# Two heads' shared query tile weighed by the whole TensorE array, each head in a PSUM slot of its own

## The chip, the cores and the metric

The kernel runs on one core of a Trainium2 chip. The metric is the device time of one execution in microseconds (us). Before the change the median of three runs is 1435.6 us (1434.48 to 1436.16).

## What is computed

Three layers stand one behind the other. The first is attention over 4 batches and 8 heads with 1152 keys of 64 numbers, where neighbouring pairs of queries are averaged, so that 576 queries per head are left. Its output, 2304 rows of 512, goes through two feed-forward layers (512 to 2048 to 512), one with `h * cos(h)`, one with `h * sigmoid(h)`.

```python
q_pool = q.reshape(B, H, S // 2, 2, D).mean(axis=3)
scores = scale * np.matmul(q_pool, k.transpose(0, 1, 3, 2))
scores = scores - np.max(scores, axis=-1, keepdims=True)
attn = np.exp(scores)
attn = attn / (np.sum(attn, axis=-1, keepdims=True) + 1e-09)
x = np.matmul(attn, v)            # 576 queries x 64 for each of 32 heads
h = x_rows @ w_in;  g = h * np.cos(h);  y = g @ w_out          # layer 1
h = y @ w_in2;      g = h / (1 + np.exp(-h));  out = g @ w_out2 # layer 2
```

## The kernel before, in words

**Pairs and tiles.** The 32 heads are worked in 16 pairs. A head has 576 = 4 x 128 + 64 queries: four whole tiles of 128 queries, and half a tile. The two halves of a pair share one tile, so that a pair has nine tiles: eight of one head each and one, number 8 (`2 * NT`), whose rows 0 to 63 are queries of the first head and rows 64 to 127 queries of the second. There are 144 tiles in all.

**The way of a tile.** `tile_scores` multiplies the queries with the keys on TensorE (PE) into PSUM (`sp`; lines 390, and 398 for the shared tile). `tile_exp` moves the scores out on VectorE (DVE, line 409) and takes the exponential on ScalarE (ACT, line 417). `tile_hi` and `tile_lo` split the result into two float16 parts (`hl`; ACT line 423, GpSimd (POOL) line 428), and a DMA issued by SyncE (SP, line 430) transposes them into `hlT`. Four tiles later `tile_pv` (line 434) weighs the values: 9 chunks of 128 keys times three products of high and low parts, 27 matmuls of 64 or 65 columns into `pv` (line 442). Column 65 of `vt` is ones, so that the sum of the weights comes out beside the weighted values.

**The shared tile in `tile_pv`.** Its 128 columns of weights are cut into two halves. The loop of line 439 first runs all 27 matmuls with columns 0 to 63 of `hlT` as stationary operand and the first head's values, into partitions 0 to 63 of its slot, and then 27 with columns 64 to 127 and the second head's values, into partitions 64 to 127. That is 54 matmuls on half the array's columns. The score products of the shared tile (line 398) are cut in the same way, with the two heads taking turns.

**Groups.** Five tiles (`GT`) share one PSUM tile `pv`, one slot of 65 numbers each; a pair has a group of five, whose last is the shared tile, and a group of four. `group_end` (line 448) divides by the sums: two small DVE instructions make the reciprocals (lines 451, 455), and line 461 multiplies each destination: `x` for whole tiles, `xrem` for the shared one. There is one `pv` buffer, so the next group's first product waits for the last of these.

**The order.** The program is written tile by tile. Between tiles a generator puts in units of layer 1 (`g1_unit` line 518, `g2_unit1` line 578, 12 matmuls of 256 columns each) at a fixed rate once the first block of attention is done. The framework then orders each engine's instructions by priority and by simulated times; `tile_pv` has a lower urgency (`P_PV = -100`), so that its matmuls are mixed with those of layer 1 on PE. Each engine then works its list strictly in order. After the last tile come the rest of layer 1, with the second layer's weights being decoded, and layer 2 (lines 518 and 599).

Of the kernel before, what the change touches and what calls it, by code (L numbers as in the profile page):

```python
# [11 lines left out]
F32 = mybir.dt.float32  # L12
# [28 lines left out]
GT = 5  # L41
# [3 lines left out]
def attention_moe_moe_kernel(ctx, tc, q, k, v, w_in1, w_out1, w_in2, w_out2, out):  # L45
# [4 lines left out]
    B, H, S, D = q.shape  # L50
# [6 lines left out]
    NT = SQ // 128  # L57
# [5 lines left out]
    small = ctx.enter_context(tc.tile_pool(name="small", bufs=2))  # L63
# [49 lines left out]
    @contextmanager  # L113
    def ahead(n):

        at_ = tc.cur_priority
        tc.cur_priority = at_ - n
        yield
        tc.cur_priority = at_ + (tc.cur_priority - (at_ - n))
# [147 lines left out]
    def att_pools(stack):  # L267
        at = Weights()
        at.p = stack.enter_context(tc.tile_pool(name="att", bufs=2, side="right", reuse_waits="tile"))
        at.src_stack = ExitStack()  # L270
        at.src = at.src_stack.enter_context(tc.tile_pool(name="src", bufs=2, side="right", reuse_waits="tile"))
        at.ps_s = stack.enter_context(tc.tile_pool(name="ps_s", bufs=1, space=PSUM, side="right"))
        at.ps_v = stack.enter_context(tc.tile_pool(name="ps_v", bufs=1, space=PSUM, side="right"))
        return at
# [102 lines left out]
    def tile_scores(at, P, t):  # L377


        T = Pair()  # L380
        T.P, T.t = P, t

        parts = [(0, 512), (512, S)]
        T.sp = [(a, z, at.ps_s.tile([128, z - a], F32, tag="sp%d" % a, name="sp")) for a, z in parts]
        if t < 2 * NT:
            kT = P.kT[t // NT]
            for a, z, sp in T.sp:
                for o, n in segs:
                    for e in range(2 if a <= o < z else 0):
                        nc.tensor.matmul(  # L390
                            sp[:, o - a:o - a + n], P.qT[e][:, t, :], kT[:, o:o + n], start=(e == 0), stop=(e == 1)
                        )
        else:
            for a, z, sp in T.sp:
                for o, n in segs:
                    for e in range(2 if a <= o < z else 0):
                        for i in range(2):
                            nc.tensor.matmul(
                                sp[i * 64:(i + 1) * 64, o - a:o - a + n], P.qT[e][:, t, i * 64:(i + 1) * 64],
                                P.kT[i][:, o:o + n], start=(e == 0), stop=(e == 1),  # L400
                            )
        return T
# [31 lines left out]
    def tile_pv(at, T):  # L434
        P, t, G = T.P, T.t, T.G
        if T.gi == 0:
            G.pv = at.ps_v.tile([128, GT, D + 1], F32, tag="pv", name="pv")
        hs = [(slice(0, 128), t // NT)] if t < 2 * NT else [(slice(0, 64), 0), (slice(64, 128), 1)]
        for r, i in hs:
            for c in range(KC):  # L440
                for e, z, n in ((0, 0, D + 1), (0, 1, D), (1, 0, D + 1)):
                    nc.tensor.matmul(  # L442
                        G.pv[r, T.gi, 0:n], T.hlT[:, e, c, r], P.vt[i][:, c, z, 0:n],
                        start=(c == 0 and e == 0 and z == 0), stop=(c == KC - 1 and e == 1),
                        skip_group_check=True,
                    )

    def group_end(at, G, n, dsts):

        den = small.tile([128, GT, 1], F32, tag="den", name="den", bufs=2)  # L450
        nc.vector.tensor_scalar(
            out=den[:, 0:n], in0=G.pv[:, 0:n, D:D + 1], scalar1=1e-9 * 2.0**PSH, scalar2=G.P.s[:, 2:3],
            op0=ALU.add, op1=ALU.mult,
        )
        nc.vector.reciprocal(den[:, 0:n], den[:, 0:n])
        for o, shape, dst in dsts:
            k = math.prod(shape)
            src, d = G.pv[:, o:o + k, 0:D], den[:, o:o + k].to_broadcast([128, k, D])
            if len(shape) == 2:
                src, d = (x.rearrange("p (t a) d -> p t a d", a=shape[1]) for x in (src, d))  # L460
            nc.vector.tensor_tensor(out=dst, in0=src, in1=d, op=ALU.mult)
# [154 lines left out]
    if True:  # L616
# [3 lines left out]
        xrem = wpool.tile([128, B, NP * D], F32, name="xrem")  # L620

        att_stack = ExitStack()
        at = att_pools(att_stack)
# [19 lines left out]
        def finish(g):  # L643
            while g in bg:
                advance()
# [45 lines left out]
        P = {}  # L691
# [36 lines left out]
        def x_of(b, i):  # L728
            if (b, i) not in x32:
                if (b - 1, i) in xgens:  # L730
                    finish(xgens[b - 1, i])
                x32[b, i] = wpool.tile([128, 2, DM], F32, tag="x32_%d" % i, name="x32")
            return x32[b, i]

        def block_done(b, i):
            if state.mp is None:
                finish(wg)
                wst_stack.close()
                state.mp = moe_pools(moe_stack)
            xgens[b, i] = block_steps(b, i)  # L740
            bg.append(xgens[b, i])

        def drain_pv():
            T = inflight.pop(0)
            G = T.G
            with ahead(P_PV):
                tile_pv(at, T)
            if T.gi < len(G.tiles) - 1:
                return
            b, j = T.P.b, T.P.j  # L750
            dsts = []
            if j < NP - 1:
                h = j + (G.tiles[0] // NT) * NP
                for i in range(2):
                    dsts.append((2 * i, (2,), x_of(b, i)[:, :, h * D:(h + 1) * D]))
            else:
                x = x_of(b, G.tiles[0] % NT // 2).rearrange("p t (a h d) -> p t a h d", a=2, d=D)
                dsts.append((0, (2, 2), x[:, :, :, j, :]))
            if G.tiles[-1] == 2 * NT:
                dsts.append((len(G.tiles) - 1, (1,), xrem[:, b:b + 1, j * D:(j + 1) * D]))  # L760
            group_end(at, G, len(G.tiles), dsts)
            if j == NP - 1:
                left[b] = left.get(b, set(range(2 * NT))) - set(G.tiles)
                for i in range(2):
                    if (b, i) not in gone and all(t % NT // 2 != i for t in left[b]):
                        gone.add((b, i))
                        block_done(b, i)
# [3 lines left out]
        for n, (b, j) in enumerate(pairs):  # L771
# [7 lines left out]
            for o in range(0, len(seq), GT):  # L779
                G = Pair()  # L780
# [9 lines left out]
            for idx, (G, gi, t) in enumerate(order):  # L790
                with ahead(P_SC):
                    T = tile_scores(at, P[n], t)
                T.G, T.gi = G, gi
                inflight.append(T)
                with ahead(P_EX):
                    tile_exp(at, T)
                tile_hi(at, T, b == 0 or (idx % HI_N) < HI_A)
                tile_lo(at, T)
                advance()
                share(RATE[b] / 2)  # L800
                advance()
                if len(inflight) > LAG:
                    drain_pv()
                advance()
                share(RATE[b] / 2)
                advance()
        while inflight:
            drain_pv()
            share(1)
# [23 lines left out]
        for i in range(2):  # L833
            T = wpool.tile([128, B, 2, 128], F16, tag="x32_%d" % i, name="xrT")
# [124 lines left out]
```

## Time and profile before

| | us |
|---|---|
| median of 3 runs | 1435.6 |
| profiled execution, whole | 1439.78 |
| its span in the trace | 1438.0 |
| PE busy | 1189.1 (83%) |
| DVE busy | 992.8 (69%) |
| ACT busy | 736.7 (51%) |
| POOL busy | 561.3 (39%) |

The profiled execution took 1.8 us more than its span and 4.2 us more than the median of the runs. Attention goes from the start to about 885 us, with layer 1 beside it from about 280 us on; the rest of layer 1 lasts until about 1036 us, layer 2 until the end. "Granted clock" is the share of TensorE's full clock that the chip gave; it has two levels, 2.4 GHz (1.0) and 1.2 GHz (0.5). In the forms of PE's instructions, 128*128 and 128*64 are rows and columns of the array in use. A matmul's duration in the trace runs from its start to its modelled end through the pipeline, some 0.19 us even for a small one; how long it holds the engine is seen from the start of the next.

### The profile page before, as it was taken

Reading aid. Unit: us, or ns where it says so; the run is one execution under the profiler, and the core shown is the slowest. Engines: PE = TensorE matmul, PEld = TensorE weight load, DVE = VectorE, ACT = ScalarE, POOL = GpSimd, SP = SyncE. Lnnn points to the kernel's source line nnn. Section 1 sums busy time; section 2 is a strip of 40 time slices with the busy share of each in tenths; the row PEclk is TensorE's granted clock in tenths of the full one; section 3 lists DMA queues with packets and bytes.
Section 4 is the critical chain, followed back from the end, with each engine's and each line's share of the span. In section 5 each row is a group of like instructions: output and inputs, shape, how many; then the busy total and the mean of one; then the engine's idle time right before and its main releaser. Section 6 shows DMA issues by size and latency. Waiting matters only on the chain. (4 is left out here: it accounts for less than half of the span.)

```text
span 1438.0 us, 27552 instructions
## 1 busy us (share of the span) xinstructions
PE 1189.1 (83%) x11460; PEld 870.2 (61%) x11460; DVE 992.8 (69%) x1840; ACT 736.7 (51%) x763; POOL 561.3 (39%) x264
## 2 busy tenths in 40 slices
PE   1455365779988877998979989898899999999998
PEld 0233244566766655676656768777786666666665
DVE  7999987598787867987798895999833222323212
ACT  3676486477667667776667665546511111111110
POOL 1578375454556474656645552545410000000000
PEclk9986568798999998999999999989899999999999
DMA  7799889986799999997997965434210000000001
GB/s 230 191 232 199 206 161 187 207 159 111 153 210 164 198 204 185 202 162 161 182 188 144 222 102 107 123 113 132 74 60 30 15 16 30 30 30 15 16 1 30
DMA packets 493085, 186.34 MB, mean 130 GB/s; under 512 B 433056, under 2 KB 467872, under 8 KB 492960
## 3 DMA queue, kind: packets, MB, share of 16 engines
q1 hardware_dynamic: 492960, 184.59, 62.5%
q8 instruction: 89, 1.46, 0.4%
q14 instruction: 36, 0.29, 0.1%
HBM read 66.58 MB, written 9.44 MB: 53 GB/s over the span
## 5 line engine op out<-in xcount | busy, mean ns | idle before, releaser
L428 POOL TENSOR_TENSOR hl<-sc,hl 128x1152 f16<-128x1152 f32 x144 | 368.0, 2564 | 221.9 <-ACT hl L423 132.6
L442 PE MATMUL pv<-vt,hlT 128*128 128x65 f16 (+3 forms) x4320 | 253.5, 206 | 61.6 <-DMA hlT<-hl 45.2
L442 PEld LDWEIGHTS <-hlT 128*128 128x128 f16 (+1 forms) x4320 | 208.2, 108 | 119.0 <-DMA hlT<-hl 57.3
L518 PEld LDWEIGHTS <-ih 128*128 128x128 f16 x2304 | 226.4, 99 | 75.1 <-issue 14.9
L390 PE MATMUL sp<-kT,qT 128*128 128x512 f16 (+1 forms) x768 | 193.0, 366 | 95.1 <-DVE sc L409 77.7
L409 DVE TENSOR_SCALAR_CACHE_REDUCE sc<-sp,psu 128x512 f32<-128x512 f32 (+1 forms) x288 | 229.9, 808 | 52.1 <-PE sp L390 43.3
L531 ACT ACTIVATE hk<-h,ca 128x512 f32<-128x512 f32 x144 | 98.2, 683 | 326.8 <-PE h L518 326.8
L417 ACT ACTIVATE sc<-sc,nb 128x1152 f32<-128x1152 f32 x144 | 179.8, 1251 | 152.2 <-DVE nb L414 129.0
L518 PE MATMUL h<-ys,ih 128*128 128x256 f16 x1152 | 197.4, 274 | 2.9 <-ACT hk L531 2.9
L518 PE MATMUL h<-xT,ih 128*128 128x256 f16 x1024 | 190.6, 278 | 7.9 <-DVE pu__2739 L98 3.4
L423 ACT ACTIVATE hl<-sc 128x1152 f16<-128x1152 f32 x144 | 165.6, 1157 | 19.3 <-DMA hlT<-hl 11.7
L566 DVE TENSOR_SCALAR gh<-hk,ck 128x1024 f16<-128x1024 f32 x36 | 27.0, 751 | 206.9 <-PE o L599 194.2
L390 PEld LDWEIGHTS <-qT 128*128 128x128 f16 x768 | 76.3, 108 | 153.3 <-issue 112.3
L578 PE MATMUL y<-gh,oh 128*128 128x256 f16 x576 | 162.4, 282 | 4.2 <-ACT y L587 4.2
L578 PE MATMUL y<-gl,oh 128*128 128x256 f16 x576 | 162.2, 282 | 0.0
L578 PE MATMUL y<-gh,ol 128*128 128x256 f16 x576 | 162.0, 281 | 0.0
L518 PE MATMUL h<-ys,il 128*128 128x256 f16 x576 | 157.6, 274 | 0.0
L518 PE MATMUL h<-xT,il 128*128 128x256 f16 x512 | 142.7, 279 | 0.0
L559 POOL TENSOR_TENSOR gl<-tt,gh 128x1024 f16<-128x1024 f32 x36 | 87.6, 2434 | 112.7 <-DVE gh L558 82.3
L578 PEld LDWEIGHTS <-oh 128*128 128x128 f16 x1152 | 115.2, 101 | 23.8 <-issue 4.7
L518 PEld LDWEIGHTS <-il 128*128 128x128 f16 x1152 | 114.2, 99 | 18.9 <-issue 1.4
L599 PE MATMUL o<-ol,gh 128*128 128x512 f16 x288 | 109.1, 379 | 0.0
(279 smaller groups left out, 1776.6 us busy)
## 6 DMA issues: line engine op xcount, KB each, us to landing
wst<-in_moe_w_in_dram SPq DMA_DIRECT2D x16, 1024.0 KB, 6.1
wst<-in_moe_w_out_dram SPq DMA_DIRECT2D x16, 1024.0 KB, 6.1
stk<-in_k_dram SPq DMA_DIRECT2D x32, 288.0 KB, 4.1
stv<-in_v_dram SPq DMA_DIRECT2D x32, 288.0 KB, 4.1
stq<-in_q_dram SPq DMA_DIRECT2D x32, 256.0 KB, 3.2
ydr<-y SPq DMA_DIRECT2D x9, 512.0 KB, 2.6
y32b<-ydr SPq DMA_DIRECT2D x9, 512.0 KB, 3.2
out_dram<-osb SPq DMA_DIRECT2D x16, 256.0 KB, 2.1
```

What stands on the lines that cost most here:

```text
L390: nc.tensor.matmul(sp[:, o - a:o - a + n], P.qT[e][:, t, :], kT[:, o:o + n], start=(e == 0), stop=(e == 1))
L409: nc.vector.tensor_scalar(out=T.sc[:, a:z], in0=sp, scalar1=T.P.su, scalar2=None, op0=ALU.mult, op1=ALU.min, accum_out=mx[:, x:x + 1],)
L417: nc.scalar.activation(out=T.sc, in_=T.sc, func=AF.Exp, scale=-1.0, bias=nb)
L423: nc.scalar.activation(out=hi, in_=T.sc, func=AF.Copy)
L428: nc.gpsimd.tensor_tensor(out=T.hl[:, 1, :], in0=T.sc, in1=T.hl[:, 0, :], op=ALU.subtract)
L442: nc.tensor.matmul(G.pv[r, T.gi, 0:n], T.hlT[:, e, c, r], P.vt[i][:, c, z, 0:n], start=(c == 0 and e == 0 and z == 0), stop=(c == KC - 1 a ...
L518: nc.tensor.matmul(hp, wt[:, c, f * 128:(f + 1) * 128], xt(c), start=(i == 0), stop=(i == 3 * NC - 1), skip_group_check=True,)
L531: nc.scalar.activation(out=o, in_=blk.hp, func=AF.Copy if first else AF.Silu, scale=blk.c.a[:, g:g + 1])
L559: nc.gpsimd.tensor_tensor(out=G.gl, in0=t, in1=gh, op=ALU.subtract)
L566: nc.vector.tensor_scalar(out=gh, in0=hk, scalar1=blk.c.k, scalar2=None, op0=ALU.mult)
L578: nc.tensor.matmul(blk.y[:, oc, :], wt[:, f, oc * 128:(oc + 1) * 128], gt[:, f % 4, :], start=(f == 0 and e == 0 and oc % 2 == 0), stop=(f ...
L599: nc.tensor.matmul(blk.y[i], gt[:, f % 4, i * 128:(i + 1) * 128], wt[:, f, :], start=(f == 0 and e == 0), stop=(f == NF - 1 and e == 2),)
```

## The change

The shared tile's stationary operand is no longer cut. All 128 columns are used twice, once with each head's values, and the two products go into two neighbouring slots of `pv`, which has six. Half of each slot is of no use (the first head's values weighed by the second head's rows, and the other way round) and isn't read. `group_end` counts six slots in the group with the shared tile, and copies `xrem` in two instructions of 64 partitions, one from each slot.

```diff
     def tile_pv(at, T):
         P, t, G = T.P, T.t, T.G
         if T.gi == 0:
-            G.pv = at.ps_v.tile([128, GT, D + 1], F32, tag="pv", name="pv")
-        hs = [(slice(0, 128), t // NT)] if t < 2 * NT else [(slice(0, 64), 0), (slice(64, 128), 1)]
-        for r, i in hs:
+            G.pv = at.ps_v.tile([128, GT + 1, D + 1], F32, tag="pv", name="pv")
+        for x, i in enumerate([t // NT] if t < 2 * NT else [0, 1]):
             for c in range(KC):
                 for e, z, n in ((0, 0, D + 1), (0, 1, D), (1, 0, D + 1)):
                     nc.tensor.matmul(
-                        G.pv[r, T.gi, 0:n], T.hlT[:, e, c, r], P.vt[i][:, c, z, 0:n],
+                        G.pv[:, T.gi + x, 0:n], T.hlT[:, e, c], P.vt[i][:, c, z, 0:n],
     def group_end(at, G, n, dsts):
-        den = small.tile([128, GT, 1], F32, tag="den", name="den", bufs=2)
+        n += G.tiles[-1] == 2 * NT
+        den = small.tile([128, GT + 1, 1], F32, tag="den", name="den", bufs=2)
-        for o, shape, dst in dsts:
+        for o, shape, dst, r in dsts:
             k = math.prod(shape)
-            src, d = G.pv[:, o:o + k, 0:D], den[:, o:o + k].to_broadcast([128, k, D])
+            src, d = G.pv[r, o:o + k, 0:D], den[r, o:o + k].to_broadcast([r.stop - r.start, k, D])
...
             if G.tiles[-1] == 2 * NT:
-                dsts.append((len(G.tiles) - 1, (1,), xrem[:, b:b + 1, j * D:(j + 1) * D]))
+                for i in range(2):
+                    r = slice(i * 64, (i + 1) * 64)
+                    dsts.append((len(G.tiles) - 1 + i, (1,), xrem[r, b:b + 1, j * D:(j + 1) * D], r))
```

The first place is PE's list in the middle of the shared tile of the fourteenth pair, where its products alternate with layer 1's second product (`y`, line 578). Numbers behind a name tell buffers of the same name apart; 64x65 is partitions by columns of the output. Before:

```order
L442 MATMUL pv_9382<-vt_8768,hlT_9365 64x65
L578 LDWEIGHTS oh1_83
L578 MATMUL y_8297<-gh_8514,oh1_83 128x256
L442 LDWEIGHTS hlT_9365
L442 MATMUL pv_9382<-vt_8768,hlT_9365 64x65
L578 LDWEIGHTS oh1_83
L578 MATMUL y_8297<-gl_8515,oh1_83 128x256
```

And now, where line 441 is the matmul of `tile_pv`:

```order
L441 MATMUL pv_9395<-vt_8780,hlT_9378 128x65
L578 LDWEIGHTS oh1_83
L578 MATMUL y_8309<-gh_8526,oh1_83 128x256
L441 LDWEIGHTS hlT_9378
L441 MATMUL pv_9395<-vt_8780,hlT_9378 128x64
L578 LDWEIGHTS oh1_83
L578 MATMUL y_8309<-gl_8527,oh1_83 128x256
```

The place in the list is the same within two rows and the alternation stays; only the form of the product is another. Through the whole of PE's list the number of matmuls stays at 11,394.

The second place is the shared tile of the ninth pair (`hlT_5643`), where the list itself differs. Before, layer 1's first product (`h`, line 518) comes in between:

```order
L442 MATMUL pv_5661<-vt_5150,hlT_5643 64x64
L442 LDWEIGHTS hlT_5643
L442 MATMUL pv_5661<-vt_5150,hlT_5643 64x65
L518 LDWEIGHTS ih1_81
L518 MATMUL h_6009<-xT_5412,ih1_81 128x256
L442 LDWEIGHTS hlT_5643
L442 MATMUL pv_5661<-vt_5150,hlT_5643 64x65
```

Now the 54 products stand in one piece, and layer 1's behind them:

```order
L441 MATMUL pv_5669<-vt_5188,hlT_5651 128x65
L441 LDWEIGHTS hlT_5651
L441 MATMUL pv_5669<-vt_5188,hlT_5651 128x64
L441 LDWEIGHTS hlT_5651
L441 MATMUL pv_5669<-vt_5188,hlT_5651 128x65
L518 LDWEIGHTS il1_82
L518 MATMUL h_6018<-xT_5420,il1_82 128x256
```

The third is DVE's list at the end of the last pair's group of five. Before:

```order
L451 TENSOR_SCALAR den_11274<-pv_10911,ps__10008 128x5
L455 RECIPROCAL den_11274<-den_11274 128x5
L461 TENSOR_TENSOR x32_8953<-pv_10911,den_11274 128x4x64
L461 TENSOR_TENSOR xrem_94<-pv_10911,den_11274 128x64
L111 TENSOR_REDUCE xm_11279<-x32_8953 128x1
```

And now:

```order
L451 TENSOR_SCALAR den_11289<-pv_10926,ps__10022 128x6
L455 RECIPROCAL den_11289<-den_11289 128x6
L461 TENSOR_TENSOR x32_8965<-pv_10926,den_11289 128x4x64
L461 TENSOR_TENSOR xrem_94<-pv_10926,den_11289 64x64 x2
L111 TENSOR_REDUCE xm_11295<-x32_8965 128x1
```

One more instruction (`x2`) and one more element in the two before it; the order around it is the same here.

## Rows read from the trace of the kernel before

**Rows 1.** Windows by stage: length, busy us of five engines, clock, DMA, GB/s.
```profile
core 0: us, PE busy (x) PEld busy (x) DVE busy (x) ACT busy (x) POOL busy (x), PEclk, DMA share, GB/s
0.00:250.00 250.00, 119.92 (x1254) 76.55 (x1254) 223.88 (x460) 156.05 (x149) 137.49 (x69) 0.78 0.91 201
250.00:350.00 100.00, 78.77 (x809) 58.66 (x810) 78.52 (x147) 62.94 (x63) 48.42 (x23) 0.85 0.83 155
350.00:650.00 300.00, 254.19 (x3052) 191.08 (x3050) 239.00 (x502) 212.00 (x211) 176.70 (x87) 0.94 1.02 187
650.00:885.00 235.00, 205.29 (x2439) 156.71 (x2437) 193.24 (x365) 155.67 (x158) 123.80 (x57) 0.97 0.87 163
885.00:1036.00 151.00, 134.83 (x1139) 115.43 (x1137) 141.76 (x210) 85.04 (x91) 68.51 (x27) 0.93 0.36 105
1036.00:1438.00 402.00, 396.05 (x2776) 271.75 (x2775) 116.39 (x161) 65.03 (x93) 6.37 (x3) 0.99 0.08 26
```

**Rows 2.** Waits from 350 to 885 us: total, times, longest.
```profile
PE sp L390 <- DVE sc L409: 39.2, 30, 4.3
DVE sc L409 <- PE sp L390: 30.7, 28, 4.5
...
PE pv L442 <- DMA hlT<-hl: 17.4, 7, 3.8
DVE den L451 <- PE pv L442: 14.7, 4, 5.4
```

**Rows 3.** PE's timeline, unmixed products: start, length, form, count.
```profile
129.52 1.80 PE L442 MATMUL pv<-vt,hlT 128*64 128x65 f16 x54 [2.37 <-DMA hlT<-hl]
...
499.88 1.00 PE L442 MATMUL pv<-vt,hlT 128*128 128x65 f16 x27
```

**Rows 4.** PE's timeline in the ninth pair's shared tile.
```profile
502.63 0.22 PE L442 MATMUL pv<-vt,hlT 128*64 128x65 f16 x1
502.78 0.28 PE L518 MATMUL h<-xT,ih 128*128 128x256 f16 x1
502.99 0.22 PE L442 MATMUL pv<-vt,hlT 128*64 128x64 f16 x1
503.14 0.28 PE L518 MATMUL h<-xT,il 128*128 128x256 f16 x1
```

**Rows 5.** PE's timeline in a whole tile mixed with layer 1.
```profile
583.99 0.19 PE L442 MATMUL pv<-vt,hlT 128*128 128x65 f16 x1
584.02 0.27 PE L578 MATMUL y<-gh,oh 128*128 128x256 f16 x1
584.13 0.19 PE L442 MATMUL pv<-vt,hlT 128*128 128x65 f16 x1
584.16 0.27 PE L578 MATMUL y<-gl,oh 128*128 128x256 f16 x1
```

**Rows 6.** PE's timeline in stretches at half clock, shared tile, then whole tile.
```profile
325.27 0.26 PE L442 MATMUL pv<-vt,hlT 128*64 128x65 f16 x1
...
325.79 0.26 PE L442 MATMUL pv<-vt,hlT 128*64 128x64 f16 x1
...
546.23 0.26 PE L442 MATMUL pv<-vt,hlT 128*128 128x65 f16 x1
...
546.50 0.26 PE L442 MATMUL pv<-vt,hlT 128*128 128x65 f16 x1
```

**Rows 7.** Groups of DVE instructions at the end of a group: busy us, mean ns.
```profile
L461 DVE TENSOR_TENSOR x<-pv,den 128x128 f32<-128x128 f32 x48 | 11.6, 281 | 0.2
...
L461 DVE TENSOR_TENSOR xrem<-pv,den 128x64 f32<-128x64 f32 x16 | 3.4, 213 | 0.0
...
L455 DVE RECIPROCAL den<-den 128x5 f32<-128x5 f32 x16 | 3.0, 184 | 0.2
...
L455 DVE RECIPROCAL den<-den 128x4 f32<-128x4 f32 x16 | 2.7, 169 | 0.1
```

**Rows 8.** DVE's timeline, a wait for a shared tile.
```profile
668.83 0.23 DVE L451 TENSOR_SCALAR den<-pv,ps__6982 128x5 f32<-128x5 f32 x1 [5.25 <-PE pv L442]
```

**Rows 9.** PE's timeline, scores of a shared tile, the heads taking turns.
```profile
727.12 0.73 PE L398 MATMUL sp<-kT,qT 128*64 128x512 f16 x8
```

More of the change, by code (lines that the diff above doesn't have):

```diff
@@ L754, in drain_pv @@
                 for i in range(2):
-                    dsts.append((2 * i, (2,), x_of(b, i)[:, :, h * D:(h + 1) * D]))
+                    dsts.append((2 * i, (2,), x_of(b, i)[:, :, h * D:(h + 1) * D], slice(0, 128)))
             else:
                 x = x_of(b, G.tiles[0] % NT // 2).rearrange("p t (a h d) -> p t a h d", a=2, d=D)
-                dsts.append((0, (2, 2), x[:, :, :, j, :]))
+                dsts.append((0, (2, 2), x[:, :, :, j, :], slice(0, 128)))
             if G.tiles[-1] == 2 * NT:
-                dsts.append((len(G.tiles) - 1, (1,), xrem[:, b:b + 1, j * D:(j + 1) * D]))
+                for i in range(2):
+                    r = slice(i * 64, (i + 1) * 64)
+                    dsts.append((len(G.tiles) - 1 + i, (1,), xrem[r, b:b + 1, j * D:(j + 1) * D], r))
             group_end(at, G, len(G.tiles), dsts)
```

## Prediction

> **What bounds the kernel now.** I read the windows by stage first, because the change touches only attention. From 1036 us on nothing is touched: PE is busy for 396 of 402 us with layer 2 [rows 1]. From 885 to 1036 us there is no product of attention either. In the first 250 us PE is busy for 120 us of 250 and DVE for 224: DVE sets the pace there. From 250 us on layer 1 shares PE with attention. From 350 to 885 us, 535 us long, PE is busy for 254.2 + 205.3 = 459.5 us (86%) and DVE for 239.0 + 193.2 = 432.2 us (81%); ACT and POOL are behind. So PE is the fullest engine of that stretch, with DVE not far below. The table of waits then shows who is late: DVE waits for score products 30.7 us and for `pv` at a group's end 14.7 us, PE waits for DVE to empty the scores 39.2 us and for the transposed weights 17.4 us [rows 2]. The two engines hold each other up. What is taken off PE there is worth something, but not its whole length.
>
> **The products themselves.** Their number stays at 54 per shared tile, 16 tiles, and so do their columns. In one piece, 54 half products take 1.80 us: after the last one's 0.22 us (its length in [rows 4]), (1.80 - 0.22) / 53 = 30 ns from one to the next. 27 full products take 1.00 us, (1.00 - 0.19) / 26 = 31 ns [rows 3, 5]. So half the array is neither faster nor slower, and this edit costs nothing: 54 x 1 ns = 0.05 us a tile, 0.9 us over 16 at the most.
>
> The Trainium skill has a rule that speaks against the change (TensorEngine Tiling (Array Packing), Key Properties): different tiles of the array load and multiply independently, at the same time. The trace agrees where two heads take turns: eight score products, four of 512 and four of 128 columns, end in 0.73 us [rows 9], less than they could one behind another. It doesn't hold in `tile_pv`, where one head's 27 come before the other's and the pace is that of full products. By that rule, 54 half products would take as long as 27 full ones, and the change would add 27 x 30 ns = 0.8 us a tile.
>
> **Going from one form to the other.** This is the large term, and the timeline shows it. In the shared tile half products alternate with layer 1's full ones, and the period of the two together is 502.99 - 502.63 = 0.36 us [rows 4]. Where a whole tile alternates with layer 1's equally long products it is 584.13 - 583.99 = 0.14 us [rows 5]. The start times show on which side: from a full product of 256 columns to the half one 0.21 us instead of 0.11, and from the half one to the full one 0.15 instead of 0.03. PE loses 0.224 us for each time that it goes to the half form and back. At half clock it is 0.52 against 0.27 us [rows 6], 0.25 us lost; so it hardly depends on the clock. The waits don't show it, since PE counts as busy throughout.
>
> How often: counted through PE's list, `tile_pv` enters the half form 160 times before and never after. In the timeline, some 5 of these fall before 250 us, 15 in 250 to 350, 60 in 350 to 650 and 80 in 650 to 885. A dozen single switches come behind a wait, which hides them; that leaves about 154 there-and-backs, x 0.224 = 34.5 us. The scores of the shared tile keep the half form; they are entered 53 times before and 48 after, 5 x 0.224 = 1.1 us less. Together PE gets some 35 us of work less, 31 of them from 350 to 885 us. The bounds of this term are 31 us (the switches cost what was counted only in that stretch) and 37 (the waiting ones count as well).
>
> **DVE's added work.** `xrem` takes two instructions in place of one. No row shows one over 64 partitions; the same 64 columns over 128 partitions take 213 ns [rows 7], so I take 213 for each, between 107 (if it halved with the partitions) and 281 (an `x` copy of twice its columns). One more slot costs the reciprocal 184 - 169 = 15 ns [rows 7], and I give its neighbour 5. That is 16 x (213 + 20) = 3.7 us; with the bounds, 0.3 to 5.9 us. The next group's first product waits for the last of these, since `pv` has one buffer; behind it on PE stand scores and layer 1, so 0.23 us a pair may be on the path. Where DVE is late it counts, and I put 40% of it on the path: 1.5 us.
>
> **How much of PE's 35 us reaches the end.** An upper bound: PE is busy for 86% of the stretch, and in the other 14% its speed doesn't matter: 30 us. A lower bound is from who waits for whom: DVE waits for PE (30.7 + 14.7 = 45.4 us) about as long as PE for DVE (39.2) [rows 2], so PE is the late one in 45.4 / 84.6 = 54% of such meetings: 19 us. There are direct cases: once the end of a group's products keeps DVE idle for 5.25 us [rows 8]. I take 60%, near the lower end, since DVE at 81% has to do the same work in less time.
>
> **The clock.** PE's granted clock was 0.78 where PE was busy for 48% of the time, 0.85 at 79%, 0.94 at 85% and 0.97 at 87% [rows 1]. With 31 us less work in a stretch some 19 us shorter, PE would be busy for 428.5 of 516 us, 83%. Some of the time lost in switches counts as busy now without being products, so I expect little: 0.01 of the clock, 428.5 x 0.01 / 0.95 = 4.5 us of PE's time given back.
>
> **Sum.** (35 - 4.5) x 0.6 = 18.3 us less, 1.5 us more on DVE: 16.8 us less. The profiled execution's 1439.8 us would become 1423.0. It lies 4.2 us above the median of the runs, and I predict for the latter: 1435.6 - 16.8 = 1418.8, said as 1419. Its own range is 8 to 26 us less, 1410 to 1428.
>
> **Rivals.**
> - *Nearly all of it arrives.* PE is the bound of the whole stretch; DVE's 103 us of idle time from 350 to 885 us close up. Then 35 us less, with the 14% off and DVE's cost in the shade: 1435.6 - 30 = 1406, to 1400 if the shorter waits on `pv` (14.7 us) help too. For it: PE is 86% busy, and DVE ran at 90% in the first 250 us. Against it: 39.2 us of waits for DVE.
> - *It is absorbed.* PE reaches its next wait for DVE or for the transposed weights earlier and waits longer: 17.4 us of waits for the DMA, whose engines are at 1.02 of their share from 350 to 650 us [rows 1]. Then only what stands before 45.4 us of DVE's waits moves, at 20%: 7 us less and 1.5 more, 1430. That the order on every engine shifts somewhat is in here; it can move the end by a few us either way.
> - *Slower, by the clock.* With PE less full its clock falls over 350 to 885 us to the 0.85 that it had at 250 to 350 us, where it was busy for 79%. PE's 428.5 us of work at 0.95 become 428.5 x 0.95 / 0.85 = 479 us, 19 more than now; 60% of that is 12, and DVE's 1.5 on top: 1449. It decides from a mean clock of 0.89 downwards (428.5 x 0.95 / 459.5). Against it: the time in switches is not products, so PE does as many products in less time, and at 650 to 885 us, with most switches, the clock was the highest.
> - *Slower, by the array's halves.* If half products ran side by side, the change would add 0.8 us x 16 = 13 us of PE's time, 8 of them on the path: 1444. That result comes from the skill's rule above; the pace of 30 ns in [rows 3] denies it.
>
> The Trainium skill (TensorE: Matmul & The Clock Gate, Part 1) says that the throttled clock is the default and activity releases it. The stages' clocks in [rows 1] rise with PE's busy share, as it says; whether time lost between forms counts as activity no row here shows, and by it the clock rival would have its chance.
>
> **How the numbers follow.** My forecast's own case 58%, nearly all 17%, absorbed 15% (of which a third within the bound of no change), slower by the clock 5%, by the array's halves 1%, and 4% for an order that happens to be bad, mostly slower. A measurement of this kernel tells 0.2%, 2.9 us, from no change. Faster by more: 58 + 17 + 10 = 85%, and 1 of the bad order: 86%. The same: 5 + 1 = 6%. Slower: 8%. The range that leaves out 2 in 10 reaches from 1401, which leaves out the best of the second case, to 1431, which leaves out the slower cases and the weak end of the absorbed one.
>
> **What would show it.** In the trace of the changed kernel no product of line 441 has the form 128*64, and a product of the shared tile with one of layer 1 has a period of 0.14 us at full clock. PE's busy time falls by about 30 to 35 us, to some 1155 to 1160, nearly all before 885 us, and attention ends some 17 us before the 885 us of now. The stretches behind it stay at 151 and 402 us. DVE's `xrem` takes 32 instructions. DVE's wait for `pv` falls below 14.7 us, and PE's wait for DVE's scores grows above 39.2. The prediction is wrong in its size if PE's busy time falls as said and its idle time grows by as much; in its mechanism if the period of the alternation stays at 0.36; in its clock if PEclk from 350 us to the end of attention is under 0.92.

## The result

The changed kernel takes 1421.8 us (median of 4 runs, 1420.0 to 1423.2) against 1435.0 us for the kernel before: a ratio of 0.991 (95% interval 0.9891 to 0.9928), 13 us less. The prediction was 1419 us, between 1401 and 1431, faster with 86%. The forecast was 16.8 us less, 13.2 came. The profiled execution of the changed kernel is the shortest of its four (1420.0 us, span 1418.2) and that of the kernel before was long (1439.8, span 1438.0), so the two traces differ by 19.8 us; what is compared between traces below is a few us more than the medians show.

The list of `tile_pv`'s products, as the answer on its line gives it: duration ns (least, median, most), first and last start, forms. First before, then after:

```profile
L442 PE MATMUL pv<-vt,hlT x4320: 190/194/264, 49.2 to 882.0; 128*128 128x65 f16 x105, 128*128 128x64 f16 x52, 128*64 128x65 f16 x27, 128*64 128x64 f16 x13
```

```profile
L441 PE MATMUL pv<-vt,hlT x4320: 190/193/262, 48.7 to 861.1; 128*128 128x65 f16 x131, 128*128 128x64 f16 x66
```

The half form (128*64) is gone, and the last product starts 20.9 us earlier. The timeline of PE in the changed kernel, where products of attention and of layer 1 alternate in the fourteenth pair (start, length):

```profile
792.90 0.19 PE L441 MATMUL pv<-vt,hlT 128*128 128x65 f16 x1
792.93 0.27 PE L578 MATMUL y<-gh,ol 128*128 128x256 f16 x1
793.04 0.19 PE L441 MATMUL pv<-vt,hlT 128*128 128x64 f16 x1
793.07 0.27 PE L578 MATMUL y<-gh,oh 128*128 128x256 f16 x1
```

The period is 0.14 us, as it was for whole tiles [rows 5], and not the 0.36 us of [rows 4]. The windows by stage of the changed kernel, whose stages after 650 us begin where the corresponding work does (columns as in [rows 1]):

```profile
0.00:250.00 250.00, 122.45 (x1254) 78.18 (x1254) 222.41 (x462) 155.20 (x149) 135.01 (x69) 0.77 0.91 200
250.00:350.00 100.00, 76.20 (x836) 58.14 (x837) 81.64 (x156) 65.94 (x66) 48.75 (x23) 0.88 0.86 165
350.00:650.00 300.00, 252.40 (x3182) 195.19 (x3180) 254.94 (x530) 220.73 (x223) 185.43 (x90) 0.93 1.03 194
650.00:865.00 215.00, 181.08 (x2289) 145.29 (x2286) 178.13 (x345) 144.73 (x145) 113.10 (x53) 0.95 0.90 164
865.00:1016.00 151.00, 129.97 (x1131) 112.06 (x1130) 141.11 (x209) 85.19 (x92) 68.50 (x26) 0.97 0.36 105
1016.00:1418.00 402.00, 396.40 (x2776) 271.98 (x2775) 116.24 (x161) 64.98 (x93) 6.37 (x3) 0.99 0.07 26
```

The two stages behind attention keep their 151 and 402 us. All of the gain lies before. The waits of the changed kernel from 350 us to the end of attention (us, times, longest) answer to [rows 2]:

```profile
PE sp L390 <- DVE sc L409: 43.5, 29, 3.4
DVE sc L409 <- PE sp L390: 22.6, 22, 4.0
PE pv L441 <- DMA hlT<-hl: 15.1, 10, 2.9
...
DVE den L451 <- PE pv L441: 1.9, 1, 1.9
```

DVE waits 8.1 us less for scores and 12.8 us less for the products at a group's end; PE waits 4.3 us more for DVE. One window from 350 us to the end of attention says it in a row, first before, then after:

```profile
350.00:882.00 532.00, 456.49 (x5460) 345.11 (x5458) 429.34 (x861) 367.67 (x369) 298.64 (x142) 0.96 0.96 177
```

```profile
350.00:861.00 511.00, 429.47 (x5430) 336.87 (x5428) 429.68 (x866) 365.45 (x367) 296.40 (x142) 0.94 0.99 183
```

PE is busy for 27.0 us less. DVE is busy for as long as before, 429 us; what went is 21.3 us of its idle time (102.7 to 81.3), 20.9 of it the two waits for PE above. In DVE's terms, the change took off waits and not work. The same sum can be made for PE (27.0 us less work, 6.0 us more idle time), so it doesn't say by itself which engine decides.

### The profile page after: what moved, and what is told of

Its sections match the earlier page's. It is cut to its first block, busy times and chain, and to the rows that moved or that the text cites. A ratio compares the mean times of both kernels' runs of the same rounds, so it can differ in the third digit from the quotient of the medians.

```text
span 1418.2 us, 27581 instructions
## 1 busy us (share of the span) xinstructions
PE 1158.5 (82%) x11460; PEld 860.8 (61%) x11460; DVE 994.5 (70%) x1856; ACT 736.8 (52%) x763; POOL 557.2 (39%) x264
## 5 line engine op out<-in xcount | busy, mean ns | idle before, releaser
L428 POOL TENSOR_TENSOR hl<-sc,hl 128x1152 f16<-128x1152 f32 x144 | 363.3, 2530 | 218.3 <-ACT hl L423 155.9
L441 PE MATMUL pv<-vt,hlT 128*128 128x65 f16 (+1 forms) x4320 | 247.7, 205 | 62.3 <-DMA hlT<-hl 46.2
L390 PE MATMUL sp<-kT,qT 128*128 128x512 f16 (+1 forms) x768 | 199.2, 379 | 102.6 <-DVE sc L409 84.5
L518 PEld LDWEIGHTS <-ih 128*128 128x128 f16 x2304 | 226.6, 99 | 74.8 <-issue 14.7
L441 PEld LDWEIGHTS <-hlT 128*128 128x128 f16 x4320 | 211.6, 106 | 94.9 <-DMA hlT<-hl 57.6
L518 PE MATMUL h<-xT,ih 128*128 128x256 f16 x1024 | 185.6, 277 | 3.7 <-DVE pu__2743 L98 2.5
L578 PE MATMUL y<-gh,oh 128*128 128x256 f16 x576 | 159.0, 276 | 1.8 <-ACT y L587 1.7
L578 PE MATMUL y<-gl,oh 128*128 128x256 f16 x576 | 159.3, 277 | 0.0
```

The source lines that it names most:

```text
L390: nc.tensor.matmul(sp[:, o - a:o - a + n], P.qT[e][:, t, :], kT[:, o:o + n], start=(e == 0), stop=(e == 1))
L428: nc.gpsimd.tensor_tensor(out=T.hl[:, 1, :], in0=T.sc, in1=T.hl[:, 0, :], op=ALU.subtract)
L441: nc.tensor.matmul(G.pv[:, T.gi + x, 0:n], T.hlT[:, e, c], P.vt[i][:, c, z, 0:n], start=(c == 0 and e == 0 and z == 0), stop=(c == KC - 1 ...
L518: nc.tensor.matmul(hp, wt[:, c, f * 128:(f + 1) * 128], xt(c), start=(i == 0), stop=(i == 3 * NC - 1), skip_group_check=True,)
L578: nc.tensor.matmul(blk.y[:, oc, :], wt[:, f, oc * 128:(oc + 1) * 128], gt[:, f % 4, :], start=(f == 0 and e == 0 and oc % 2 == 0), stop=(f ...
```

## The experiments

Each was timed against the kernel before on the same chip. Two kernels are compared by the difference of their ratios, times 1436 us; by the intervals of the ratios, such a difference is known to some 3 to 5 us.

**Theory** as the runs began: the time lost in going between the half and the full form is what the change saves, and some 40% of PE's time reaches the end. **Rivals**: the order of the lists or the two slots bring it; half products are slower by themselves. After the first four runs the share itself was in doubt, and a second theory came in: PE's time counts little, and the switches cost because they stretch the last tile of a group, for which DVE waits.

| run | what it is | median us | ratio (95%) | against before |
|---|---|---|---|---|
| | changed kernel | 1421.8 | 0.9910 (0.9891 to 0.9928) | -13 |
| E1 | two slots, half products | 1436.0 | 0.9993 (0.9983 to 1.0004) | -1 |
| E2 | half products in one piece | 1408.7 | 0.9807 (0.9794 to 0.9820) | -28 |
| E3 | full products in one piece | 1416.2 | 0.9855 (0.9841 to 0.9870) | -21 |
| E4 | changed, products done twice | 1426.5 | 0.9930 (0.9913 to 0.9948) | -10 |
| E5 | E2 with two xrem instructions | 1421.3 | 0.9883 (0.9855 to 0.9912) | -17 |
| E6 | E2, heads taking turns | 1411.7 | 0.9818 (0.9793 to 0.9843) | -26 |
| E7 | E3 with one xrem instruction | 1411.3 | 0.9809 (0.9784 to 0.9834) | -27 |
| E8 | E6, scores urgent too | 1421.7 | 0.9875 (0.9847 to 0.9903) | -18 |
| E9 | changed, switches put in layer 1 | 1421.2 | 0.9891 (0.9873 to 0.9910) | -16 |
| E10 | before, shared tile first | 1411.2 | 0.9824 (0.9802 to 0.9847) | -25 |
| E11 | changed, shared tile first | 1414.0 | 0.9840 (0.9819 to 0.9861) | -23 |
| E12 | changed, another order | 1422.6 | 0.9904 (0.9886 to 0.9922) | -14 |

### E1: the half form put back into the changed kernel

```diff
+            r = slice(0, 128) if t < 2 * NT else slice(x * 64, (x + 1) * 64)
...
+                    s = slice(0, 128) if c == e == z == 0 else r
...
-                        G.pv[:, T.gi + x, 0:n], T.hlT[:, e, c], P.vt[i][:, c, z, 0:n],
+                        G.pv[s, T.gi + x, 0:n], T.hlT[:, e, c, s], P.vt[i][:, c, z, 0:n],
```

> The changed kernel with its two slots, its six-slot reciprocals and its two xrem instructions, but with the shared tile's products on half the array again (all but the first of each head's 27). PE's list enters the half form 144 times for them (160 before the change, 0 after). Theory (the time lost in going between the forms is what the change saved): about the kernel before, -2 to +3 us against it, PE busy 1185 to 1192 us. Rival (the gain is from the shifted order or from the slots, not from the form): as fast as the changed kernel, 11 to 15 us under the kernel before, PE busy near 1160.

Measured: 0.9993, as slow as the kernel before. The engines' line of its page (busy us, share, instructions):

```profile
PE 1194.4 (83%) x11460; PEld 873.0 (61%) x11460; DVE 1001.4 (70%) x1856; ACT 734.8 (51%) x761; POOL 561.1 (39%) x264
```

PE's busy time is back at 1194 us, just above what was expected (changed kernel: 1158.5). The gain needs the full form; slots and DVE's instructions don't bring it. The rival falls.

### E2 and E3: the shared tile's products in one piece

```diff
-            with ahead(P_PV):
+            with ahead(P_PV if T.t < 2 * NT else 400):
                 tile_pv(at, T)
```

In E2 this is done to the kernel before:

> The kernel before, half products and one slot, but the shared tile's 54 products get a high urgency, so that they stand in one piece in PE's list: 16 entries into the half form instead of 160 (the scores' entries rise from 53 to 68). Theory (only the alternation costs, the half form doesn't): 144 - 15 = 129 there-and-backs x 0.224 = 29 us of PE's time less, PE busy about 1160, and 10 to 19 us under the kernel before. Rival (the half products are slower in themselves, or the slots matter): no gain, within 4 us of the kernel before.

Measured: 0.9807, 28 us under the kernel before, more than was expected, and 15 under the changed kernel. PE busy 1165.5 us. Half products are no slower in themselves; what cost was their alternation with full ones. In E3 it is done to the changed kernel:

> The changed kernel with the same high urgency for the shared tile's products: the control for the order that the urgency brings. Theory: no form change is taken away (the scores' entries rise from 48 to 59, 11 x 0.224 = 2.5 us of PE's time), so within 4 us of the changed kernel, 9 to 16 us under the kernel before. Rival (standing in one piece is what helps, whatever the form): clearly faster than the changed kernel, 20 us or more under the kernel before.

Measured: 0.9855, 8 us under the changed kernel and 21 under the kernel before: the rival's branch, if only just. So the urgency brings something that has nothing to do with the form of the shared tile's products, and as much of E2's 28 us may be of that kind. Full products in one piece are 7 us behind half ones (E2). The next runs ask why.

### E4: the shared tile's products twice

```diff
-            for c in range(KC):
+            for c in list(range(KC)) * (1 if t < 2 * NT else 2):
```

> The changed kernel with every product of the shared tile done twice (the second pass writes over the first): 864 more full products at 30 ns, 26 us more work on PE, none elsewhere, no form change. It measures how much of PE's time reaches the end. Theory (about half of it): 11 to 18 us over the changed kernel, so within 5 us of the kernel before. Rival A (PE is the bound, all of it arrives): 23 us or more over the changed kernel, 10 us over the kernel before. Rival B (absorbed): under 5 us over the changed kernel.

Measured: 0.9930, 3 us over the changed kernel, from 864 products more, 26 us at their pace. That is rival B. But PE's busy time grew by 15.9 us only (1174.4 against 1158.5), and its granted clock over the execution was 0.934 in place of 0.922. A share of 40% is excluded for the 26 us; for the 15.9 it would be 6 us, which the intervals just allow. From 350 us to the end of attention (one window, columns as in [rows 1]):

```profile
350.00:871.00 521.00, 439.54 (x6025) 350.90 (x6024) 428.94 (x866) 362.76 (x363) 297.06 (x142) 0.95 0.96 178
```

DVE is busy for 429 us once more. PE's busy time in this stretch grew by 10 us, with a clock of 0.95 in place of 0.94.

### E5 and E7: DVE's added work by itself

E5 adds the second `xrem` instruction to E2 (the edit of `group_end`, which takes the partitions `r`, isn't shown):

```diff
-                dsts.append((len(G.tiles) - 1, (1,), xrem[:, b:b + 1, j * D:(j + 1) * D]))
+                for i in range(2):
+                    r = slice(i * 64, (i + 1) * 64)
+                    dsts.append((len(G.tiles) - 1, (1,), xrem[r, b:b + 1, j * D:(j + 1) * D], r))
```

> The kernel with half products in one piece (28 us under the kernel before), with the change's second xrem instruction added: xrem copied in two instructions of 64 partitions from its one slot, 16 x 0.22 = 3.4 us more on DVE, nothing else. It measures DVE's added work by itself. Theory (DVE is late about as often as PE; this work sits between a group's last product and the next group's first): 2 to 5 us over the kernel without it, 23 to 26 us under the kernel before. Rival A (it is hidden): within 1.5 us of the kernel without it. Rival B (it explains all of the 7.6 us by which full products in one piece are behind half products in one piece): 6 to 9 us over it.

Measured: 0.9883, 11 us over E2, above both branches. E7 takes the change's added instruction and slot out of E3:

```diff
-        n += G.tiles[-1] == 2 * NT
...
-                for i in range(2):
-                    r = slice(i * 64, (i + 1) * 64)
-                    dsts.append((len(G.tiles) - 1 + i, (1,), xrem[r, b:b + 1, j * D:(j + 1) * D], r))
+                dsts.append((len(G.tiles) - 1, (1,), xrem[:, b:b + 1, j * D:(j + 1) * D], slice(0, 128)))
```

> Full products in one piece, with DVE's added work taken out again: reciprocals of five slots and one xrem instruction, which reads the first of the two slots for both heads, so that the second head's rows of the shared tile aren't the reference's. It tells the slots' DVE work from the form of the products. Theory (the 7.6 us between full and half products in one piece are DVE's work): 1408 to 1411, 26 to 29 us under the kernel before. Rival (full products cost more, or the order differs): 1414 to 1418, like full products in one piece.

Measured: 0.9809, 7 us under E3 and level with E2, as the theory had it. So in these orders 16 instructions of 216 ns come with 7 to 11 us, two or three times their own length. Adding an instruction also moves others in the list (over a hundred of DVE's instructions stand elsewhere in either pair of traces), and which of the two costs the time was not separated.

### E6 and E8: less of PE's time

E6 is E2 with the heads taking turns, so that neighbouring half products use different halves of the array:

```diff
-        for r, i in hs:
-            for c in range(KC):
-                for e, z, n in ((0, 0, D + 1), (0, 1, D), (1, 0, D + 1)):
+        for c in range(KC):
+            for e, z, n in ((0, 0, D + 1), (0, 1, D), (1, 0, D + 1)):
+                for r, i in hs:
```

> Half products in one piece, with the two heads taking turns product by product instead of one head behind the other, so that neighbours use different halves of the array. If they run side by side, as the scores' do, a tile's 54 products take 27 x 30 ns, 0.8 us less, 13 us of PE's time over 16 tiles, and no engine else has less work. Theory (40% of PE's time reaches the end): 4 to 7 us under half products in one piece, 32 to 35 under the kernel before. Rival A (PE's time is absorbed, as the doubled products suggested, 18%): 2 to 3 us under it. Rival B (they don't run side by side): no difference, PE busy the same.

Measured: 0.9818, not faster than E2. The engines' line of its page:

```profile
PE 1150.7 (81%) x11460; PEld 847.3 (60%) x11460; DVE 990.4 (70%) x1840; ACT 734.4 (52%) x761; POOL 560.2 (40%) x264
```

PE is busy for 14.8 us less than in E2 (1165.5), so the halves do run side by side, as the Trainium skill says (TensorEngine Tiling (Array Packing), Key Properties). 40% of that would be 6 us less at the end; 2 us more were measured. But DVE's instructions took longer in this order: 730.8 us from the start to the end of attention, against 722.9 in E2 with one instruction fewer. So the run doesn't show what PE's time alone is worth. E8 makes the shared tile's scores urgent as well:

```diff
-                with ahead(P_SC):
+                with ahead(P_SC if t < 2 * NT else 400):
                     T = tile_scores(at, P[n], t)
```

> As the kernel with half products taking turns in one piece, and the shared tile's score products urgent too: these enter the half form 29 times instead of 66. 37 x 0.224 = 8.3 us of PE's time less. Theory (40% of it): 2 to 5 us under the kernel without that urgency, 35 to 39 under the kernel before. Rival (the switches of the scores stand where PE waits for DVE anyway): no difference. Other rival (scores put ahead delay other tiles' scores): slower.

Measured: 0.9875, 8 us over E6, though PE is busy for 1145.9 us, the least of all. It is slower, as the last rival had it, but not for its reason: DVE waits no longer for scores than in E6 (23.1 us against 25.2 from 250 us to the end of attention). DVE's busy time from the start to the end of attention is 738.0 us in place of 730.8, with 1466 instructions in both, and attention ends 8 us later.

### E9: the same switches at another place

```diff
-                nc.tensor.matmul(
-                    hp, wt[:, c, f * 128:(f + 1) * 128], xt(c), start=(i == 0), stop=(i == 3 * NC - 1),
...
+                for z in [slice(0, 64), slice(64, 128)] if w is W1 and i == 6 else [slice(0, 128)]:
+                    nc.tensor.matmul(
+                        hp[z], wt[:, c, f * 128 + z.start:f * 128 + z.stop], xt(c),
...
```

> The changed kernel, with switches put back at another place: in each of layer 1's first products one of the 12 matmuls is done as two of half the array, 152 entries into the half form, none of them in the shared tile's products. 152 x 0.224 = 34 us more on PE, as much as the change took away, some two thirds of it before the end of attention. Theory 1 (PE's time counts wherever it is saved, about 40% of it): 10 to 16 us over the changed kernel, about the kernel before. Theory 2 (the time counts where the shared tile's last product keeps DVE waiting at the group's end, and is mostly absorbed elsewhere): 0 to 6 us over the changed kernel.

Measured: 0.9891, as fast as the changed kernel. PE's timeline shows that the switches are there; the x3 are the two halves and the next full product, run together by the view:

```profile
624.71 0.27 PE L519 MATMUL h<-xT,il 128*128 128x256 f16 x1
624.92 0.52 PE L519 MATMUL h<-xT,ih 128*64 128x256 f16 x3
625.27 0.27 PE L519 MATMUL h<-xT,il 128*128 128x256 f16 x1
```

From one `il` to the next it is 0.56 us; three products of 0.109 us would be 0.33. The difference, 0.23 us, is the price of [rows 4] again, with the halves side by side. Of the stretch from 350 us to the end of attention:

```profile
350.00:861.00 511.00, 437.89 (x5485) 324.90 (x5483) 428.30 (x865) 363.21 (x363) 295.19 (x140) 0.95 0.97 182
```

Its length is that of the changed kernel to the microsecond; PE fills 8.4 us more of it, and DVE is busy for 428 us. Over the whole execution PE is busy for 18.1 us more (1176.6 against 1158.5) and not for 34; the granted clock was 0.935 in place of 0.922, which by an estimate from these numbers (1176.6 x 0.013 / 0.922) makes up for some 17 us. 40% of 18.1 us would be 7 us; 3 us less than the changed kernel were measured. Theory 1 falls: PE's time is not worth 40% wherever it is spent. But the waits don't follow theory 2 either. In this stretch DVE waits 9.2 us longer than in the changed kernel for scores and 3.1 longer at a group's end, and the end doesn't move:

```profile
DVE sc L409 <- PE sp L390: 31.8, 29, 3.8
...
DVE den L451 <- PE pv L441: 5.0, 5, 3.5
```

### E10 and E11: the shared tile not at the group's end

```diff
-            seq.insert(NT, 2 * NT)
+            seq.insert(0, 2 * NT)
```

with the destinations counted accordingly. E10 is the kernel before with it, half products mixed with layer 1:

> The kernel before, half products mixed with layer 1, but the shared tile is the first of its pair and of its group of five, so that no group's end follows right behind it. Its products enter the half form 78 times (160 before): 82 x 0.224 = 18 us less on PE. Theory 1 (40% of PE's time): 5 to 9 us under the kernel before. Theory 2 (DVE's wait at the group's end is what the switches cost): 10 to 16 us under it, and DVE's wait for pv falls from 18.4 us to 5 or less, with the other half of the switches still there.

Measured: 0.9824, 25 us under the kernel before. PE is busy for 1169.8 us. DVE's waits from 250 us to the end of attention:

```profile
DVE sc L409 <- PE sp L390: 35.7, 30, 8.2
...
DVE sc L409 <- PE sp L398: 11.4, 7, 3.4
...
DVE den L451 <- PE pv L442: 4.3, 2, 2.5
```

The wait at the group's end is down to 4.3 us there (18.2 in the kernel before in that stretch), though one of 6.1 us before 250 us makes it 10.4 in all, more than expected. The gain is larger than either theory gave. And the waits for scores rose, from 34.0 and 5.1 us to 35.7 and 11.4, so that the three together fell by 5.9 us only. The wait at the group's end can't be all of the gain. E11, the control:

> The changed kernel with the shared tile first, the control for the run with half products: no switch of the shared tile is there to be moved. Theory 1 and 2: within 4 us of the changed kernel. Rival (the order of the tiles is worth something by itself): 5 us or more away from it.

Measured: 0.9840, 10 us under the changed kernel: the rival. The tile's place is worth something by itself, and it had not been known. With the shared tile first, half products with 78 entries into the half form are as fast as full ones with none (0.9824 against 0.9840), which fits theory 2. It doesn't show it, because E11 also carries the second `xrem` instruction and the sixth slot and E10 doesn't. At 40%, the 78 entries would be worth 78 x 0.224 x 0.4 = 7 us, and DVE's added work, which came with 7 to 11 us in E5 and E7, could hide that. A run with full products, the shared tile first and one `xrem` instruction would have told.

### E12: another order of the same work

```diff
-P_CH, P_SC, P_EX, P_PV, P_MS, P_MU, P_W, P_PR, P_X = 0, 60, 0, -100, 200, 0, 0, 0, 0
+P_CH, P_SC, P_EX, P_PV, P_MS, P_MU, P_W, P_PR, P_X = 0, 60, 0, -70, 200, 0, 0, 0, 0
```

> The changed kernel with a slightly higher urgency of all products of attention's second step (-70 in place of -100): the same instructions, another order (659 of DVE's 1538 rows stand elsewhere). It measures what the order alone moves. If it is within 2 us of the changed kernel, differences of 5 us between the other runs are those of the work; if it is 5 us or more away, differences of that size between runs with different orders say nothing on the work.

Measured: 0.9904, 1 us under the changed kernel. One reordering that moved 659 rows moved the time by nothing that can be told. It is one sample: E11 and E3 reorder too, and gain 8 to 10 us.

## Why the prediction was right, and where a term was off

**The products cost nothing: right.** E2 keeps them on half the array and is the fastest of all.

**The switches: right.** Period and form are as forecast. PE's busy time fell from 1189.1 to 1158.5 us, 30.6 us; 30 to 35 were forecast. E1 brings them back with the form alone. The Trainium skill names a cause that fits (TensorEngine Tiling (Array Packing), Key Properties): a change of tiling mode, not of the tile, drains the engine. It gives no time. Here it is 0.22 us for a there-and-back in the kernel before, and 0.23 in E9.

**The share of 60%: near in size, its reason not shown.** Between medians 13.2 of 30.6 us arrived, 43%, or 48% with the 1.5 us for DVE put back; my lower bound was 54%. Between the two traces it is 19.8, 65%, but one of these executions was long and the other short. That the number came out near is in part luck. The step treated PE's time as one coin: so much less work on the fuller engine, a part of it at the end. E9 puts 18.1 us of PE's time elsewhere and loses nothing, E4 adds 15.9 and loses 3, E6 takes 14.8 off and gains nothing, though DVE's work grew there.

A reading that fits part of this is theory 2: the switches counted because they stand in the last tile of a group of five, whose end DVE waits for in order. [rows 8] was one such wait; I had that row and used it as an example of the share. For this reading: DVE is busy for 429 us before and after the change, and of the 20.9 us by which its two waits fell, 12.8 are at a group's end. Against it: in E1, as slow as the kernel before, that wait is 11.6 us from 250 us on, where the kernel before has 18.2 and the changed kernel 4.9; in E9 the waits grew at no cost; and E10 gained 25 us while the waits for PE fell by 5.9. So it is shown that the half form costs time where it is mixed with the full one (E1 mixes it in again, E2 keeps it unmixed); on which path the time reaches the end is argued, not shown.

**DVE's own work wasn't constant.** I took it as the same work in less time. Windows from the start to the end of attention hold the same work, but for the `xrem` instructions. In one trace of each (columns as in [rows 1]): the kernel before, the changed kernel, E1, E2, E10.

```profile
0.00:882.00 882.00, 655.17 (x7520) 480.32 (x7521) 731.74 (x1466) 586.65 (x580) 484.55 (x234) 0.89 0.93 181
0.00:861.00 861.00, 628.12 (x7518) 473.19 (x7519) 733.72 (x1482) 586.59 (x580) 480.16 (x234) 0.88 0.95 186
0.00:880.00 880.00, 663.14 (x7514) 484.97 (x7515) 741.84 (x1482) 585.95 (x579) 484.74 (x234) 0.88 0.93 182
0.00:851.00 851.00, 634.03 (x7519) 471.47 (x7520) 722.90 (x1465) 583.34 (x577) 486.27 (x234) 0.88 0.96 188
0.00:854.00 854.00, 639.75 (x7522) 471.45 (x7523) 717.29 (x1465) 583.43 (x577) 483.93 (x234) 0.88 0.95 187
```

DVE is busy for 8.8 us less in E2 and 14.5 less in E10 than in the kernel before, and for 8.1 more in E1 than in the changed kernel, with as many instructions but for one. So the same instructions took longer or shorter from trace to trace, whose orders differ: the 36 of line 543 alone range from 0.68 to 2.85 us in the kernel before. What sets their length no run tested. It is a part of what E2 and E10 gain beyond the waits, and of E8's loss. It is also 8 of the 19 us by which attention ends later in E1 than in the changed kernel, so how much of E1's loss is the switches' own is open.

**DVE's added work: perhaps mis-sized on the path.** Its own length was right. The groups of the changed kernel (busy us, mean ns), which answer to [rows 7]:

```profile
L461 DVE TENSOR_TENSOR xrem<-pv,den 64x64 f32<-64x64 f32 x32 | 6.9, 216 | 0.2
...
L455 DVE RECIPROCAL den<-den 128x6 f32<-128x6 f32 x16 | 3.0, 186 | 0.2
```

An instruction over 64 partitions takes 216 ns, no less than one over 128 (213); the sixth element costs the reciprocal 2 ns, not 15. That is 3.5 us in all. I put 1.5 us of it on the path; E5 and E7 say 11 and 7 in their orders. In E1, which has the same added work and 16 entries fewer than the kernel before, nothing is seen of it, and E11 is 2 us behind E10. So it is between 0 and 11 us, by the order around it, and my bound of 5.9 us may be too low; what part of the 11 is the instruction's and what the order's is open.

**The clock: small, as said.** It went from 0.96 to 0.94 from 350 us to the end of attention; 0.01 was forecast, 0.92 the mark for being wrong. My series of clocks against busy shares left out a row of [rows 1]: from 885 to 1036 us PE was busy for 89% at a clock of 0.93, under the 0.97 at 87%. So the rows don't rise in step throughout.

**The rest.** The stretches behind attention kept their length, DVE's wait for `pv` fell below 14.7 us (to 1.9), PE's wait for DVE's scores rose above 39.2 (to 43.5), attention ended 21 us earlier in the trace, where 17 were forecast. None of the rivals came in.

**What stays open.** Why urgency for the shared tile (E3 against the changed kernel, 8 us) and its place at the front (E11, 10 us) help where the shared tile's products have no form change left; what sets the length of DVE's instructions; and whether E5's 11 us are the instruction or the order that it brings. E2 is the best of all runs: half products, one slot, high urgency, 1408.7 us, 15 us under the changed kernel by the ratios.

## What to carry to other kernels

One behind another, products on half the array's columns cost as much as those on all of them (30 and 31 ns), but going to that form and back costs 0.22 us of PE, and the waits of a profile don't show it, since PE counts as busy: read it from start to start in the timeline. Before widening such products, try to keep them together: one word of urgency (E2) gave twice the gain of the change, though 8 of its 28 us may be the order's (E3).

Time taken off the fullest engine is not worth a fixed share: some 34 us of switches at another place, 18.1 us of PE's busy time, cost nothing (E9). Put the same work back at another place before you believe a share, and compare the busy time of the other engines over the same work: DVE's moved by 14 us with the place of a tile alone (E10).

## What was not expected of the hardware

The half-form switch costs about the same at half clock, 0.25 us [rows 6]. Half products of two heads run side by side when they take turns (E6: 14.8 us less PE time), and didn't when one head's came behind the other's (30 ns for each, [rows 3]). A DVE instruction over 64 partitions takes as long as one over 128 (216 and 213 ns). In the two runs that add work on PE to the changed kernel the granted clock was higher (0.922 there, 0.934 in E4, 0.935 in E9), and PE's busy time grew by less than the work added (15.9 us of 26, 18.1 of 34). E1, with its switches in the shared tile, had 0.920.
